# Issuing the second copy of x behind the stores instead of ahead of them, in a state-attention and Mish-MLP kernel

## The chip, the core and the metric

The kernel runs on one core of a Trainium2 chip. The metric is the device time of one launch in microseconds (us). The kernel before takes 706.17 us, the median of three runs (705.65 to 708.63). One further execution, of 704.28 us, was recorded by the hardware profiler; all profile lines are from it, and their times count from the start of its span of 702.3 us.

## The reference

Eight batches b of eight heads, each with 512 tokens of x (width 64) and 32 state rows. The tokens read from the state and the state reads from the tokens, by two softmaxes over the same scores; the results are stacked to 544 rows per batch and go through a two-layer network with the activation h * tanh(softplus(h)), called Mish.

```python
scores = scale * np.matmul(x, state.transpose(0, 1, 3, 2))
a = softmax(scores)                      # over the 32 state rows
xread = np.matmul(a, state)
scores2 = scale * np.matmul(state, x.transpose(0, 1, 3, 2))
a2 = softmax(scores2)                    # over the 512 tokens
sread = np.matmul(a2, x)
attn = np.concatenate([xread, sread], axis=2)      # (8, 8, 544, 64)
h = attn_as_rows @ w_in                  # (4352, 512) @ (512, 2048)
out = mish(h) @ w_out                    # (2048, 512)
```

Everything is float32 (softmax is short for the max, exp, sum and division of the reference).

## The kernel before, in words

**Work per batch.** `attention(b)` makes the softmax weights of batch b as pieces that are issued between the other work; a batch's attention runs one batch ahead. The network's hidden width of 2048 is cut into 8 slots `(b, j)` of two blocks of 128. In a slot, `sw_slice` (L377) multiplies the state into `w_in`, `gemm1` (L416) gives the 512 tokens' hidden values in two PSUM tiles `ph` (12 matmuls), ScalarE applies Mish (`g`, L394), VectorE splits `g` into `gh` and `gl` (L399, L400), and `gemm2` (L470, 24 matmuls) adds to four accumulators `acc` of 512 tokens in PSUM. Numbers are split into a high and a low part and multiplied in three matmuls. `gemm2` runs two slots behind `gemm1` (LAG).

**End of a batch.** After the eighth slot the four accumulators are copied to SBUF tiles `o` of which there are two: VectorE copies the even ones (L477), ScalarE the odd ones (L479), and SP issues a store of each to DRAM (L485). The third and fourth copy need a tile `o` whose store has landed. Because of the lag, this falls into slot 1 of the next batch.

**Two copies of x.** The token read needs x as it lies (`x`, L72, one tile). The scores need x transposed. For batches 0 and 1 TensorE transposes it. For batches 2 to 7 a second copy `xq` is loaded in blocks of 32x32 (L85, 32 DMAs of 32 KB for each batch), and VectorE transposes it in four instructions to `xT` (L197), one for each pair of heads c and c+4. The 32 DMAs go through the eight heads in turn, so chunk c of four is complete with DMA 20, 24, 28 or 32. `xq` takes a tile of the pool `raw` (two tiles, shared with the raw weights in the first batch, and with `ws` in the stage for the state rows, L432).

**What sets the order.** The Tile framework puts the program in order for each engine by a simulated timeline, and inserts the waits that the data and the buffers need. An engine's instructions then run in that order. `behind(m)` keeps what is issued in it from being placed before the instruction last marked `m`. All DMAs but three of the first state are issued from SP's one queue: a DMA there that waits for a buffer holds up all that stand behind it.

**Where `xq` is issued.** In the main loop, in batch `key`, `xq` of batch `key + 2` is issued in slots 6 and 7 (batch 0) or 2 to 5 (the others), behind the mark "mish", the last Mish activation.

In DMA and tile names a number after the name tells batches apart: `xq_1057` is batch 2, `xq_1371` batch 3, `xq_2026` batch 4; `o_0_1299` to `o_3_1326` are the results of batch 0, `o_0_1954` to `o_3_1981` of batch 1.

Of the kernel before, what the change touches and what calls it, by code (L numbers as in the profile page):

```python
# [39 lines left out]
def state_attention_mish_kernel(ctx, tc, x, state, w_in, w_out, out):  # L40

    nc = tc.nc
# [97 lines left out]
    def split_w_out(j, w):  # L140
        wo[j] = const.tile([P, 2, 2, DM], F32R, tag=f"wo{j}", name=f"wo_{j}")
        nc.vector.tensor_copy(wo[j][:, :, 1], w)
        last["wo"] = nc.vector.tensor_sub(wo[j][:, :, 0], w, as_f32(wo[j][:, :, 1]))  # L143
# [25 lines left out]
    last = {}  # L169

    @contextmanager
    def behind(*marks):

        with ExitStack() as st:
            for m in marks:
                st.enter_context(tc.issue_after(last[m].ins if hasattr(last[m], "ins") else last[m]))
            yield
# [228 lines left out]
    def gemm1(b, j, aT, sw):  # L406
        swh, swl = sw[j]
        phs = []
        for k in range(2):
            ph = ps_h.tile([P, 512], F32, tag="ph", name=f"ph_{b}_{j}_{k}")  # L410
            seq = []
            for kc in range(2):
                hi, lo = aT[kc]
                seq += [(swh[:, k, kc], hi), (swh[:, k, kc], lo), (swl[:, k, kc], hi)]
            for i, (l, r) in enumerate(seq):
                last["PE"] = nc.tensor.matmul(ph, l, r, start=(i == 0), stop=(i == len(seq) - 1))  # L416
            phs.append(ph)
        return phs
# [8 lines left out]
    def load_w_s(j):  # L427
        w = pool.tile([P, NC, 2, 2 * P], F32, tag="raw", name=f"ws_{j}", bufs=2)
        f0 = 2 * j * P
        for kc in range(2):  # L430
            for r in range(2):
                nc.sync.dma_start(  # L432
                    w[half(kc), :, r], w_in_sb[half(r), kc * NC:(kc + 1) * NC, f0:f0 + 2 * P])
        return w

    def gemm1_s(j, ws):

        g = new_g(f"s_{j}")
        ph = [ps_h.tile([P, 512], F32, tag="ph", name=f"ph_s_{j}_{r}") for r in range(2)]
        for r in range(2):  # L440
            for k in range(2):
                w = ws[:, :, r, k * P:(k + 1) * P]
                hi, lo = (pool.tile([P, NC, P], F32R, tag="t", name=f"w{n}_{j}_{r}_{k}", bufs=5) for n in "hl")
                nc.scalar.copy(hi, w)
                nc.vector.tensor_sub(lo, w, as_f32(hi))  # L445
                for c in range(NC):
                    for n, (l, i) in enumerate(((hi, 0), (hi, 1), (lo, 0))):
                        nc.tensor.matmul(  # L448
                            ph[r][:, k * 256:(k + 1) * 256], l[:, c], srT[i][:, c],
                            start=(c == 0 and n == 0), stop=(c == NC - 1 and n == 2))  # L450
        for r in range(2):
            take_g(g, r, ph[r])
        return split_g(f"s_{j}", g)
# [3 lines left out]
    def new_accs(key, ntok):  # L457
        accs[key] = [ps_acc.tile([P, 512], F32, tag="acc", name=f"acc_{key}_{t}") for t in range(ntok)]

    def gemm2(key, fcs, gh, gl, ntok, ts=None):  # L460

        if key not in accs:
            new_accs(key, ntok)
        for t in ts or range(ntok):
            for i, fc in enumerate(fcs):
                col = (i * ntok + t) * P
                sl = slice(col, col + P)
                ops = [(gh, 1), (gh, 0), (gl, 1)]
                for n, (g, w) in enumerate(ops):
                    last["PE"] = nc.tensor.matmul(  # L470
                        accs[key][t], g[:, sl], wo[fc % 8][:, fc // 8, w, :],
                        start=(fc == 0 and n == 0), stop=(fc == NFC - 1 and n == 2),
                    )
            if fcs[-1] == NFC - 1:
                o = pool.tile([P, DM], F32, tag="o", name=f"o_{key}_{t}")
                if t % 2 == 0:
                    nc.vector.tensor_copy(o, accs[key][t])  # L477
                else:
                    nc.scalar.copy(o, accs[key][t])  # L479
                if key == "s":  # L480
                    for b4 in range(4):
                        r0 = (4 * t + b4) * T + S
                        nc.sync.dma_start(out[r0:r0 + NS, :], o[b4 * NS:(b4 + 1) * NS, :])
                else:
                    nc.sync.dma_start(  # L485
                        out[key * T:key * T + S, :].rearrange("(p t) e -> p t e", t=NT)[:, t, :], o)


# [53 lines left out]
    def second(ts=None, keep=False):  # L542
        k_, fcs, g_, nt = pending[0] if keep else pending.pop(0)
        gemm2(k_, list(fcs), g_[0], g_[1], nt, ts)

    for n, (key, j) in enumerate(slots):
        if key == "s":
            if j == 0:
                ws_next = load_w_s(0)
            ws, ws_next = ws_next, load_w_s(j + 1) if j + 1 < 4 else None  # L550
            g = gemm1_s(j, ws)
            pending.append((key, (2 * j, 2 * j + 1, 2 * j + 8, 2 * j + 9), g, 2))
            second()
            continue
        if j == 0 and key > 0:
            aT = nxt_aT
        if key + 1 < B and j == (3 if key == 0 else 0):
            _, pcs, nxt_aT = attention(key + 1, xs_next, sn_next, xqs.pop(key + 1, None))
            todo += pcs
        phs = gemm1(key, j, aT, sw_next)  # L560
        if (key, j) == (0, 0):
            with behind("PE"):
                sw_next = sw_slice(0, 1, P)
            with behind("swl"):
                split_w_out(0, w_0)
            rawo.pop(0)
            with behind("swh", "wo"):
                g = mish(key, j, phs)
        else:
            g = mish(key, j, phs)  # L570
        pending.append((key, (j, j + 8), g, NT))
        if key == 0 and j + 1 < SLOTS:


            if j == 1:
                with behind("PE"):
                    second((0, 1), True)
            if j:
                with behind("PE"):
                    sw_next = sw_slice(0, j + 1, P)  # L580
            if j == 1:
                with behind("mish", "gl", "swh", "swl"):
                    rest[1]()
            with behind("mish", "gl", "swh", "swl", (0, "exp2") if j else "mish"):
                make(*makes.get(j, ()))
            if j == 0:
                with behind("join"):
                    rest[0]()
            if j == 0:
                with behind("PE"):  # L590
                    fills[0](FILL[2], accs[0][NT - 1])
                load(*((k, i) for i in range(3, 6) for k in "io" if (k, i) != ("i", 3)))
                with behind("load"):
                    xs_next, sn_next = load_x(1), load_state(1)
                load(*((k, i) for i in range(6, 8) for k in "io"))
            elif j == 1:
                with behind("PE"):
                    second((2, 3))
            elif j == 3:

                for do in (lambda: second((0, 1), True), todo.pop(0), lambda: second((2, 3))):
                    with behind("PE"):
                        do()
            elif j < 6:
                with behind("PE"):
                    second()
        else:
            nb, nj = (key, j + 1) if j + 1 < SLOTS else (key + 1, 0)
            if nb < B and nj % 2 == 0:
                sw_next = sw_slice(nb, nj)  # L610
        for _ in range((0, 0, 1, 1)[j] if key == 0 and j < 4 else 1 + (key == 0)):
            if todo:
                with behind(*(("PE",) if key == 0 and j == 2 else ())):
                    todo.pop(0)()
        if key + 2 < B and j in (parts := (6, 7) if key == 0 else (2, 3, 4, 5)):

            if j == parts[0]:
                xqs[key + 2] = new_xq(key + 2)
            m = 4 * H // len(parts)
            with behind("mish"):  # L620
                load_xq(key + 2, xqs[key + 2], range((j - parts[0]) * m, (j - parts[0] + 1) * m))
        if j == SLOTS - 1 and 0 < key + 2 < B:
            with behind("mish"):
                xs_next, sn_next = load_x(key + 2), load_state(key + 2)
        if len(pending) > LAG:
            second()
# [26 lines left out]
```

## Time and profile before

| what | value |
|---|---|
| median of three runs | 706.17 us (705.65 to 708.63) |
| the profiled execution, its span | 704.28 us, 702.3 us |
| TensorE matmul (PE) busy | 683.8 us, 97% |
| VectorE (DVE) busy | 341.5 us, 49% |
| ScalarE (ACT) busy | 263.8 us, 38% |
| GpSimd (POOL) busy | 10.4 us, 1% |
| mean granted TensorE clock | 0.994 |
| DMA, share of 16 engines | 26.3% for SP's queue |

The profile tells for each engine how long it was busy, which instruction ended an idle time ("idle before <-releaser"), and for DMAs when they were issued and how long they took to land. PEld is TensorE's weight load, SPq is SP issuing DMAs, DVEq and the like are the engines' sequencers. Matmuls overlap, so the start of one to the start of the next is the better measure of their pace.

### The profile page before, as it was taken

Reading aid. Unit: us, or ns where it says so; the run is one execution under the profiler, and the core shown is the slowest. Engines: PE = TensorE matmul, PEld = TensorE weight load, DVE = VectorE, ACT = ScalarE, POOL = GpSimd, SP = SyncE. Lnnn points to the kernel's source line nnn. Section 1 sums busy time; section 2 is a strip of 40 time slices with the busy share of each in tenths; the row PEclk is TensorE's granted clock in tenths of the full one; section 3 lists DMA queues with packets and bytes.
Section 4 is the critical chain, followed back from the end, with each engine's and each line's share of the span. In section 5 each row is a group of like instructions: output and inputs, shape, how many; then the busy total and the mean of one; then the engine's idle time right before and its main releaser. Section 6 shows DMA issues by size and latency. Waiting matters only on the chain.

```text
span 702.3 us, 11259 instructions
## 1 busy us (share of the span) xinstructions
PE 683.8 (97%) x4756; PEld 530.2 (75%) x4756; DVE 341.5 (49%) x517; ACT 263.8 (38%) x418; POOL 10.4 (1%) x13
## 2 busy tenths in 40 slices
PE   8889997999999999999999999999999999999997
PEld 6766775677777777787777777777777788977785
DVE  3687595375337533663258333743374324432221
ACT  5696853343126312451236122631245123222110
POOL 0110100000000000000000000000000000000000
PEclk9999999999999999999999999999999999999999
DMA  9995833520420032102310041004010007001001
GB/s 239 261 247 155 212 48 74 132 44 1 102 71 16 1 86 41 61 1 67 56 66 0 13 110 60 1 1 120 1 61 1 1 1 180 1 1 30 1 1 60
DMA packets 84529, 46.08 MB, mean 66 GB/s; under 512 B 57600, under 2 KB 78080, under 8 KB 84480
## 3 DMA queue, kind: packets, MB, share of 16 engines
q1 hardware_dynamic: 84048, 45.27, 26.3%
q8 instruction: 37, 0.61, 0.4%
q10 hardware_dynamic: 432, 0.10, 0.1%
q14 instruction: 12, 0.10, 0.0%
HBM read 32.24 MB, written 8.91 MB: 59 GB/s over the span
## 4 chain that ended last, share of the span: by engine, by line
PE 89%; DMA 4%; SPq 2%; DVE 2%; ACT 2%; issue 1%; ACTq 0%; DVEq 0%
PE acc L470 49%; PE ph L416 24%; PE swp L377 5%; PE ph_s L448 3%; PE acc_s L470 3%; DMA wir<-in_moe_w_in_dram 3%; SPq L85 2%; PE sc L216 1%; PE srp L327 1%; PE e2p L259 1%; DMA out_dram<-o 1%; DMA sn<-in_state_dram 1%; DVE wo L143 0%; PE xTp L203 0%; DVE w L106 0%
## 5 line engine op out<-in xcount | busy, mean ns | idle before, releaser
L470 PE MATMUL acc<-wo,gh 128*128 128x512 f32 x1024 | 328.8, 402 | 0.0
L470 PEld LDWEIGHTS acc<-wo,gh 128*128 128x128 f32 x1024 | 189.6, 189 | 55.4 <-issue 12.3
L470 PE MATMUL acc<-wo,gl 128*128 128x512 f32 x512 | 201.3, 396 | 0.0
L394 ACT ACTIVATE g<-ph 128x512 f32<-128x512 f32 x128 | 74.1, 597 | 228.6 <-DVE gl L400 162.6
L399 DVE CAST gh<-g 128x1024 fp32r<-128x1024 f32 x64 | 44.2, 691 | 158.6 <-PE acc L470 145.8
L470 PEld LDWEIGHTS acc<-wo,gl 128*128 128x128 f32 x512 | 96.8, 189 | 23.2 <-issue 0.4
L416 PE MATMUL ph<-ah,swh 128*128 128x512 f32 x256 | 101.9, 399 | 7.1 <-ACT swh L388 5.2
L416 PE MATMUL ph<-al,swh 128*128 128x512 f32 x256 | 102.2, 399 | 0.0
L416 PE MATMUL ph<-ah,swl 128*128 128x512 f32 x256 | 100.2, 397 | 0.0
L400 DVE TENSOR_TENSOR gl<-g,gh 128x1024 fp32r<-128x1024 f32 x64 | 79.0, 1234 | 5.0
L389 DVE TENSOR_TENSOR swl<-swp,swh 128x512 fp32r<-128x512 f32 (+1 forms) x72 | 42.9, 625 | 54.3 <-ACT swh L388 53.7
L416 PEld LDWEIGHTS ph<-ah,swh 128*128 128x128 f32 x256 | 48.4, 189 | 20.5 <-ACT swh L388 5.9
L416 PEld LDWEIGHTS ph<-al,swh 128*128 128x128 f32 x256 | 48.4, 189 | 11.6 <-DVE al L315 0.4
L416 PEld LDWEIGHTS ph<-ah,swl 128*128 128x128 f32 x256 | 48.3, 189 | 10.7 <-DVE swl L389 0.3
L388 ACT CAST swh<-swp 128x512 fp32r<-128x512 f32 (+1 forms) x72 | 35.8, 547 | 22.7 <-PE swp L377 22.7
L377 PE MATMUL swp<-w_in_sb,bd 64*32 64x256 f32 (+1 forms) x1152 | 40.8, 358 | 2.1 <-DVE rs L248 2.0
L394 ACT ACT_TABLE_LOAD x20 | 25.7, 1283 | 30.7 <-DVE gl L400 14.1
L377 PEld LDWEIGHTS swp<-w_in_sb,bd 64*32 64x32 f32 x1152 | 18.4, 106 | 20.5 <-issue 12.4
L479 ACT COPY o<-acc 128x512 f32<-128x512 f32 x16 | 9.4, 586 | 49.2 <-PE acc L470 27.5
L477 DVE COPY o<-acc 128x512 f32<-128x512 f32 x16 | 11.0, 688 | 28.3 <-DMA out_dram<-o 22.3
L445 DVE TENSOR_TENSOR wl<-ws,wh 128x512 fp32r<-128x512 f32 x16 | 11.1, 691 | 27.3 <-PE ph_s L448 23.3
L197 DVE STREAM_TRANSPOSE xT<-xq 128x512 f32<-128x512 f32 x24 | 24.3, 1092 | 0.0
(80 smaller groups left out, 527.5 us busy)
## 6 DMA issues: line engine op xcount, KB each, us to landing
x<-in_x_dram SPq DMA_DIRECT2D x32, 256.0 KB, 4.3
wir<-in_moe_w_in_dram SPq DMA_DIRECT2D x16, 512.0 KB, 9.3
wor<-in_moe_w_out_dram SPq DMA_DIRECT2D x16, 512.0 KB, 11.8
out_dram<-o SPq DMA_DIRECT2D x32, 256.0 KB, 2.4
xq<-in_x_dram SPq DMA_DIRECT2D x192, 32.0 KB, 2.3
ws<-w_in_sb SPq DMA_DIRECT2D x16, 256.0 KB, 4.3
sn<-in_state_dram SPq DMA_DIRECT2D x21, 32.0 KB, 3.0
out_dram<-o_s SPq DMA_DIRECT2D x8, 64.0 KB, 1.7
```

The costliest lines, as they stand in the source:

```text
L85: nc.sync.dma_start(xq[q * 32:(q + 1) * 32, h % NC, h // NC], x[b, h].rearrange("(i w u) d -> u i w d", w=8, u=2)[u][:, :, dh * 32:(dh + 1 ...
L197: nc.vector.transpose(xTs[c].rearrange("p (k v i g) -> p g k v i", k=2, v=2, g=4), xq[:, c].rearrange("p k (g v) d -> p g k v d", v=2))
L377: last["PE"] = nc.tensor.matmul(pw[r][o, kc * n:(kc + 1) * n], bds[b][half(r), kc ^ r, o], w_in_sb[half(r), kc * NC + c, j * P:j * P + n], ...
L388: last["swh"] = nc.scalar.copy(hr, pr)
L389: last["swl"] = nc.vector.tensor_sub(lo[:, r].rearrange("p k f -> p (k f)"), pr, as_f32(hr))
L394: last["mish"] = nc.scalar.activation(g[:, k * 512:(k + 1) * 512], ph, AF.Mish)
L399: nc.vector.tensor_copy(gh, g)
L400: last["gl"] = nc.vector.tensor_sub(gl, g, as_f32(gh))
L416: last["PE"] = nc.tensor.matmul(ph, l, r, start=(i == 0), stop=(i == len(seq) - 1))
L445: nc.vector.tensor_sub(lo, w, as_f32(hi))
L448: nc.tensor.matmul(ph[r][:, k * 256:(k + 1) * 256], l[:, c], srT[i][:, c], start=(c == 0 and n == 0), stop=(c == NC - 1 and n == 2))
L470: last["PE"] = nc.tensor.matmul(accs[key][t], g[:, sl], wo[fc % 8][:, fc // 8, w, :], start=(fc == 0 and n == 0), stop=(fc == NFC - 1 and ...
```

## The change

The stores of results get a mark of their own, "store". `xq` is then issued behind the last store that was issued, in batches 1 to 5 (so for batches 3 to 7), and behind the last load in batch 0 (for batch 2). By slot 2 of batch `key` the last store issued is that of the fourth tile of batch `key - 1`. No instruction is added or taken away, no size is changed.

```diff
@@ gemm2
                 else:
-                    nc.sync.dma_start(
+                    last["store"] = nc.sync.dma_start(
                         out[key * T:key * T + S, :].rearrange("(p t) e -> p t e", t=NT)[:, t, :], o)
@@ the main loop
             if j == parts[0]:
                 xqs[key + 2] = new_xq(key + 2)
             m = 4 * H // len(parts)
-            with behind("mish"):
+            with behind("store" if key else "load"):
                 load_xq(key + 2, xqs[key + 2], range((j - parts[0]) * m, (j - parts[0] + 1) * m))
```

The order on SP's queue, where batch 0 ends. Before (`xN` is a count of DMAs that stand together):

```order
L85 DMA xq_1057<-in_x_dram 32x8x32 x32
L85 DMA xq_1371<-in_x_dram 32x8x32 x24
L485 DMA out_dram<-o_0_1299 128x512
L485 DMA out_dram<-o_1_1308 128x512
L85 DMA xq_1371<-in_x_dram 32x8x32 x4
L485 DMA out_dram<-o_2_1317 128x512
L485 DMA out_dram<-o_3_1326 128x512
L85 DMA xq_1371<-in_x_dram 32x8x32
L72 DMA x_1157<-in_x_dram 128x2x256 x4
```

The same place on SP's queue with the change:

```order
L85 DMA xq_1057<-in_x_dram 32x8x32 x32
L153 DMA sn_1817<-in_state_dram 128x64 x3
L485 DMA out_dram<-o_1_1308 128x512
L485 DMA out_dram<-o_0_1299 128x512
L485 DMA out_dram<-o_2_1317 128x512
L485 DMA out_dram<-o_3_1326 128x512
L85 DMA xq_1371<-in_x_dram 32x8x32 x2
L72 DMA x_1157<-in_x_dram 128x2x256 x4
L85 DMA xq_1371<-in_x_dram 32x8x32 x30
```

All four stores of batch 0 now stand ahead of batch 3's `xq`; before, 24 of its DMAs stood ahead of the first two stores and four more ahead of the last two. Three small loads of a state (`sn`) moved ahead of the stores.

On VectorE one instruction changes its place, at the same point (piece of the difference):

```order
 L335 TENSOR_SCALAR srd_1055<-srp_0_1038,rs_0_962 128x64
 L197 STREAM_TRANSPOSE xT_3_1291<-xq_1057 128x4x128
+L477 COPY o_2_1317<-acc_2_194 128x512
 L389 TENSOR_TENSOR swl_0_1114<-swp_0_0_1095,swh_0_1113 128x512
-L477 COPY o_2_1317<-acc_2_194 128x512
 L389 TENSOR_TENSOR swl_0_1114<-swp_0_1_1096,swh_0_1113 128x512
```

The copy of the third result tile stands one instruction earlier, ahead of the low part `swl` of the first half of the weights for batch 1's slot 0. TensorE, ScalarE and GpSimd keep their order.

In the batches after it SP's queue now reads as here at the end of batch 1, with the change:

```order
L153 DMA sn_3127<-in_state_dram 128x64 x3
L485 DMA out_dram<-o_0_1954 128x512
L485 DMA out_dram<-o_1_1963 128x512
L485 DMA out_dram<-o_2_1972 128x512
L485 DMA out_dram<-o_3_1981 128x512
L85 DMA xq_2026<-in_x_dram 32x8x32 x32
L72 DMA x_2467<-in_x_dram 128x2x256 x4
L153 DMA sn_3782<-in_state_dram 128x64 x3
```

Before, batch 4's `xq_2026` and batch 5's `xq_2681` both stood ahead of batch 1's stores, and batch 6's `xq_3336` right behind them; now each batch's `xq` stands behind the stores of the batch three before it.

## The prediction

> **What bounds the kernel now.** I read the page's busy times first, then who waits for whom, then the timeline of the one place where TensorE waits.
>
> ```profile
> PE 683.8 (97%) x4756; PEld 530.2 (75%) x4756; DVE 341.5 (49%) x517; ACT 263.8 (38%) x418; POOL 10.4 (1%) x13
> ```
>
> TensorE is the bound, and only time in which it stands still or runs slowly can be won. Its waits between 113 and 640 us are one row:
>
> ```profile
> PE ph L416 <- ACT swh L388: 3.9, 1, 3.9
> ```
>
> The rest of that stretch is full (busy time by stage; the first number behind the stretch's length is PE):
>
> ```profile
> 130.00:140.00 10.00, 10.00 (x66) 6.14 (x65) 3.21 (x4) 2.59 (x5) 0.00 (x0) 1.00 0.37 63
> 250.00:326.00 76.00, 76.00 (x526) 58.41 (x525) 37.35 (x59) 25.90 (x43) 0.00 (x0) 1.00 0.18 44
> 580.00:640.00 60.00, 60.00 (x360) 50.26 (x359) 22.40 (x29) 16.78 (x29) 0.00 (x0) 1.00 0.25 62
> ```
>
> So what the change can win lies at that one wait, at the start of batch 1. Its chain, from TensorE backwards. TensorE's timeline there:
>
> ```profile
> 119.18 0.39 PE L416 MATMUL ph<-al,swh 128*128 128x512 f32 x1
> 119.41 0.40 PE L416 MATMUL ph<-ah,swl 128*128 128x512 f32 x1
> 123.68 0.77 PE L416 MATMUL ph<-ah,swh 128*128 128x512 f32 x1 [3.87 <-ACT swh L388]
> 124.25 0.63 PE L416 MATMUL ph<-al,swh 128*128 128x512 f32 x1
> ```
>
> ScalarE's:
>
> ```profile
> 112.83 0.59 ACT L479 COPY o<-acc 128x512 f32<-128x512 f32 x1 [1.26 <-PE acc L470]
> 122.56 0.58 ACT L479 COPY o<-acc 128x512 f32<-128x512 f32 x1 [7.05 <-DMA out_dram<-o]
> 123.04 0.59 ACT L388 CAST swh<-swp 128x512 fp32r<-128x512 f32 x1
> ```
>
> VectorE's:
>
> ```profile
> 113.83 0.68 DVE L477 COPY o<-acc 128x512 f32<-128x512 f32 x1
> 115.54 0.70 DVE L389 TENSOR_TENSOR swl<-swp,swh 128x512 fp32r<-128x512 f32 x1
> 121.95 0.69 DVE L477 COPY o<-acc 128x512 f32<-128x512 f32 x1 [5.72 <-DMA out_dram<-o]
> ```
>
> And SP's:
>
> ```profile
> 77.06 42.27 SPq L85 DMA_DIRECT2D xq<-in_x_dram  x56
> 119.43 1.02 SPq L485 DMA_DIRECT2D out_dram<-o  x2
> ...
> 123.14 1.02 SPq L485 DMA_DIRECT2D out_dram<-o  x2
> ...
> 124.87 2.11 SPq L72 DMA_DIRECT2D x<-in_x_dram  x4
> ...
> 130.53 22.20 SPq L85 DMA_DIRECT2D xq<-in_x_dram  x32
> ...
> 198.67 1.50 SPq L153 DMA_DIRECT2D sn<-in_state_dram  x3
> 206.00 4.20 SPq L485 DMA_DIRECT2D out_dram<-o  x4
> ```
>
> The weights' second half `swh`, for which TensorE waits, stands on ScalarE behind the copy of result tile 3. That copy waits 7.05 us for a tile `o` whose store has not landed. The first two tiles were copied by 113.42 and 114.51, but SP was issuing `xq` until 119.33 and issued their stores only then; the waiting copies start 2.5 and 3.1 us later, against a landing time of:
>
> ```profile
> DMA to landing us min/median/max: 2.1/2.4/4.1
> ```
>
> The store is late because of the 24 DMAs of batch 3's `xq` ahead of it, and for no other reason that the trace shows. Later batches have their stores on time: at 206.00 SP had been free since 200.17 (198.67 + 1.50).
>
> **The change part by part.** *The idle time, removed.* Matmuls start 0.23 us apart (119.18 to 119.41), so the next was due at 119.64 and came at 123.68: 4.04 us. With the change SP is free at this point: it has 32 DMAs of batch 2's `xq` (at 0.755 us each, 42.27/56, they fill 77.06 to about 101) and the three of `sn_1817`, bounded from below by nothing and from above by the slow first rate, 3 x 0.755 = 2.3 us; done by 104, nine us before the first store is wanted. I walk the chain with durations of the rows above and a landing of 2.5 us:
> - store of tile 1, issued at 113.4, lands at 115.9; VectorE's copy of tile 2 (now ahead of `swl`) runs 115.9 to 116.6, the first `swl` 116.6 to 117.3;
> - store of tile 0, issued at 114.5, lands at 117.0; ScalarE's copy of tile 3 runs 117.0 to 117.6, `swh` 117.5 to 118.1, the second `swl` 118.1 to 118.8.
>
> What TensorE wants, and when:
>
> ```profile
> 116.38 1.07 PE L377 MATMUL swp<-w_in_sb,bd 64*32 64x256 f32 x16
> 118.03 0.65 PE L327 MATMUL srp<-x,e2T 128*32 128x64 f32 x32
> 118.61 0.50 PE L416 MATMUL ph<-ah,swl 128*128 128x512 f32 x1
> ```
>
> The accumulators are complete before 116.38, so the copies don't wait for them. `srp` at 118.03 takes the PSUM buffer that the first `swl` reads: free at 117.3, slack 0.7 us. The matmul due at 119.64 needs `swh`: there at 118.1, slack 1.5 us. So this wait goes wholly: **4.04 us**.
>
> *The slow restart, removed with it.* By stage, with the granted clock as the third number from the end:
>
> ```profile
> 123.68:126.90 3.22, 3.22 (x10) 2.48 (x10) 0.86 (x2) 2.13 (x3) 0.00 (x0) 0.51 0.69 201
> 126.90:130.00 3.10, 3.10 (x18) 2.33 (x20) 2.36 (x4) 0.74 (x3) 0.00 (x0) 0.96 1.02 312
> ```
>
> Matmuls that started every 0.23 us start every 0.43 to 0.57 us (123.68, 124.25). At a clock of 0.51, 3.22 us hold 1.58 us too much; at 0.96, 3.10 us hold 0.12 us: **1.70 us**. Without the idle time there is nothing for the clock to drop on.
>
> *What comes after.* Mish, `gh`, `gl` and the next weights follow TensorE's own results there, so they come earlier with it. VectorE and ScalarE had 5.72 and 7.05 us of idle time at this very place, which they now get back as earlier work. I find no further wait in walking to 128 us: Mish of the first `ph` ends at 120.4 (table load behind `swh`, 118.1 to 119.4), and its buffer is wanted at 121.4. I take 0. The lower bound of this term is 0, as no row shows TensorE idle that could be filled; the upper one is rival 1 below.
>
> *`xq` of batch 3, moved back.* 32 DMAs and the four of `x` go behind the stores: from about 118 at 22.20/32 = 0.69 us, plus 2.1 us for `x`, issued by 143, landed by 145.5. It is wanted at:
>
> ```profile
> 159.26 3.00 DVE L197 STREAM_TRANSPOSE xT<-xq 128x512 f32<-128x512 f32 x3
> 231.42 2.96 DVE L197 STREAM_TRANSPOSE xT<-xq 128x512 f32<-128x512 f32 x3
> 237.44 0.69 DVE L399 CAST gh<-g 128x1024 fp32r<-128x1024 f32 x1 [3.06 <-PE acc L470]
> 249.07 1.08 DVE L197 STREAM_TRANSPOSE xT<-xq 128x512 f32<-128x512 f32 x1
> ```
>
> 159.26 less 5.7 is 153.5: hidden, with 8 us to spare. Its cover are VectorE's instructions up to there.
>
> *`xq` of batches 4 to 7, moved back.* This is where the change costs cover. The stores of batch 1 are issued by 210.2 (all times of both shift alike). Chunk 2 is complete with DMA 28: 210.2 + 28 x 0.694 + 2.3 = 231.9. VectorE turns to it as its third transpose, at 231.42 + 2 x 0.99 = 233.4. Chunk 0 (DMA 20) is there at 226.4, chunk 3 (DMA 32) at 234.7 for 249.07. So 1.5 us to spare in the tightest, and behind it VectorE idles 3.06 us anyway. The landing of 2.3 us is the median here:
>
> ```profile
> DMA to landing us min/median/max: 2.1/2.3/8.2
> ```
>
> Price 0, as long as that cover holds. `x` and `sn` behind `xq` wait for buffers that come free at the same times as before, and are consumed a batch later; `ws`, the first of which moves behind batch 7's `xq`, is wanted only in the stage of the state rows, more than a batch later.
>
> *Sum.* 4.04 + 1.70 = 5.74 us. The profiled execution of 704.28 us becomes 698.5 us. The median of the three runs stands 1.89 us above that execution, so the forecast for the median is 706.17 - 5.74 = **700.4 us**. For this kernel, a change under 0.5% (3.5 us) can't be told from none; 5.7 us is 0.8%.
>
> **Rivals.** *1. A shorter wait in the same place.* VectorE's copy of tile 2 now stands ahead of `swl`, so a late store holds up both `swl` and `srp`. If stores land in their maximum of 4.1 us instead of 2.5, `swl` ends at 118.9 and `srp` is 0.9 us late, and `swh` is there at 119.8, 0.1 us late. TensorE loses about 1.0 us: 701.4 us. If the clock also drops, 1.70 us more, 703.1 us. For it: the pool's rotation ties two engines to two stores. Against it: no `xq` competes with these stores any longer. Whether the clock drops after a short wait is seen earlier in the trace:
>
> ```profile
> 44.57 0.67 PE L377 MATMUL swp<-w_in_sb,bd 64*32 64x128 f32 x32 [2.04 <-DVE rs L248]
> 44.00:46.00 2.00, 1.43 (x34) 1.17 (x35) 1.62 (x3) 1.97 (x3) 0.00 (x0) 0.81 0.91 297
> 46.00:48.00 2.00, 2.00 (x6) 1.52 (x6) 1.37 (x3) 1.98 (x5) 0.00 (x0) 0.50 0.98 247
> 107.99 0.66 PE L259 MATMUL e2p<-ident,e 128*128 128x128 f32 x4 [0.70 <-ACT e L245]
> 100.00:120.00 20.00, 19.11 (x166) 13.50 (x164) 14.22 (x27) 8.45 (x14) 0.00 (x0) 1.00 0.31 48
> ```
>
> A wait of 2.04 us was followed by a clock of 0.50, one of 0.70 us by none (1.00 over the 20 us). 1.0 us is nearer the latter, so 701.4 is the likelier of the two. The Trainium skill, TensorE: Matmul & The Clock Gate, section "What's actually happening", has the clock halved after an idle window of about 3.4 us; by it a wait of 1.0 us would cost no clock, and rival 1 would end at 701.4 alone. The trace agrees on the half (0.51 after 3.87 us) and not on the length (0.50 after 2.04 us).
>
> *2. The gain is given back.* VectorE and ScalarE, which caught up during the stall, turn out to be just in time behind it, and TensorE waits in pieces in batch 1 or later: 0 to 4 us of the 5.74 remain, 702 to 706, say 705 us. For it: VectorE has much to do between 140 and 160 (softmax of batch 2). Against it: nothing on TensorE waits in 130 to 640 us, and VectorE idles 8.13 us in front of that softmax:
>
> ```profile
> 142.41 1.31 DVE L291 STREAM_TRANSPOSE e<-scs 128x512 f32<-128x512 f32 x2 [8.13 <-ACT scs L224]
> ```
>
> *3. Not the queue.* If the copies waited for something else than the late issue, the stores would come early and the copies would not: 706 us. Against it stand the 2.5 us from issue to release.
>
> *4. Slower: `xq` late in batches 4 to 7.* VectorE runs in order; if chunk 2 is not there when it turns to it, `gh` and `gl` behind it are late, then Mish, then TensorE. With the slow issue of 0.755 us and a landing of 8.2 us (its maximum), chunk 2 is there at 210.2 + 21.1 + 8.2 = 239.5, 6.1 us late; 3.06 us are VectorE's idle time, and 3 us in each of four batches, 12 us, would reach TensorE if `gemm2`'s lag of two slots hid nothing: 700.4 + 12 = 712 us. It decides from a delivery after 236.5. For it: 1.5 us of spare time by the medians is little. Against it: later issues are at 0.694 or faster, and nothing else is on the queue then. The Trainium skill, Perfetto Trace Analysis, section "DMA Optimizations", suggests one issuing engine for inputs and another for outputs; by it loads behind stores on one queue are what to avoid, and rival 4 is how that would cost here. No run so far shows it.
>
> **How the numbers follow.** Forecast (both terms, no new wait) 0.74; rival 1 0.12, rival 2 0.08, rival 3 0.02, rival 4 0.04. Around the forecast the three runs before spread from 0.5 us below to 2.5 us above their median. Range 698.8 to 703.8: it holds the forecast with that spread, nearly all of rival 1 and a part of rival 2. Faster by over 0.5% means below 702.6: 0.72 from the forecast, 0.08 from rival 1: 0.80. Slower means above 709.7: 0.03 to 0.04, from rival 4. The rest, 0.16, is no change.
>
> **What would show it.** Right: stores of batch 0 issued at about 113.4 and 114.5; no TensorE wait over 1 us after 113; a granted clock of 1.00 from 118 to 130; the end of the span near 696.5; `xq` of batch 4 issued in one block right behind the stores of batch 1, and its transposes without an idle time in front that a DMA ends. Wrong: an idle time before `srp` or `ph` at 117 to 121 (rival 1), ScalarE or VectorE released by a store there (rival 3), TensorE waits spread over later batches (rival 2), or a row in which VectorE's `xT` waits for a DMA of `xq` and TensorE waits a few us later (rival 4).

## The result and the profile after

| | before | with the change |
|---|---|---|
| median of 10 runs on one chip | 705.29 us (702.1 to 708.63) | 699.16 us (696.36 to 702.1) |
| ratio, 95% interval | | 0.9917 (0.9891 to 0.9942) |
| the profiled execution, its span | 704.28 us, 702.3 us | 696.36 us, 694.6 us |

The change makes the kernel faster by 0.8%, and the interval leaves out 1. Two repetitions (e8, e11 below) gave 0.9911 and 0.9910. One execution of the kernel before, of 2835 us beside e1 to e4, is left out of their ratios. The forecast was 5.74 us of 706.17 us, a ratio of 0.9919. The time forecast, 700.4 us, lies 1.2 us above the measured one, of which 0.9 us is that the kernel before has a lower median over these ten runs than over the three before the prediction.

TensorE's waits are read first. This view of the kernel with the change lists who waited for whom between 40 and 130 us (us in total, how often, the longest):

```profile
PE swp L377 <- DVE rs L248: 2.0, 1, 2.0
PE ph L416 <- ACT swh L388: 1.3, 1, 1.3
PE e2p L259 <- ACT e L245: 0.7, 1, 0.7
```

All three come before 113 us and stand in the kernel before too. From 113 to 640 us the same view has no row at all; before it had one, of 3.9 us. SP's timeline of the kernel with the change (start, length, what is issued, how many):

```profile
111.07 4.20 SPq L485 DMA_DIRECT2D out_dram<-o  x4
115.32 1.24 SPq L85 DMA_DIRECT2D xq<-in_x_dram  x2
116.66 2.08 SPq L72 DMA_DIRECT2D x<-in_x_dram  x4
118.79 20.12 SPq L85 DMA_DIRECT2D xq<-in_x_dram  x30
...
197.92 4.27 SPq L485 DMA_DIRECT2D out_dram<-o  x4
202.24 21.42 SPq L85 DMA_DIRECT2D xq<-in_x_dram  x32
```

The stores now go out as soon as their tile is copied, and `xq` follows in one block. ScalarE and VectorE at the same place, with the change:

```profile
110.45 0.59 ACT L479 COPY o<-acc 128x512 f32<-128x512 f32 x1 [1.27 <-PE acc L470]
112.54 0.59 ACT L388 CAST swh<-swp 128x512 fp32r<-128x512 f32 x1 [1.49 <-PE swp L377]
114.33 0.59 ACT L479 COPY o<-acc 128x512 f32<-128x512 f32 x1 [1.20 <-DMA out_dram<-o]
115.13 0.59 ACT L388 CAST swh<-swp 128x512 fp32r<-128x512 f32 x1 [0.22 <-PE swp L377]
```

```profile
111.46 0.67 DVE L477 COPY o<-acc 128x512 f32<-128x512 f32 x1
113.28 0.69 DVE L477 COPY o<-acc 128x512 f32<-128x512 f32 x1
113.89 0.68 DVE L389 TENSOR_TENSOR swl<-swp,swh 128x512 fp32r<-128x512 f32 x1
```

ScalarE's copy of tile 3 waits 1.20 us for a store instead of 7.05, and the `swh` behind it waits for its own input. VectorE's copy of tile 2 has no idle time in front. TensorE is full from there on, at full clock (the first number behind the stretch's length is PE, the third from the end the granted clock):

```profile
113.00:120.00 7.00, 7.00 (x73) 4.85 (x72) 3.30 (x7) 3.94 (x7) 0.00 (x0) 1.00 0.64 202
120.00:130.00 10.00, 10.00 (x66) 6.37 (x65) 4.74 (x7) 2.77 (x5) 0.00 (x0) 1.00 0.46 97
140.00:640.00 500.00, 500.00 (x3396) 389.79 (x3395) 234.98 (x364) 168.31 (x283) 0.00 (x0) 1.00 0.17 43
```

**Where the 7.7 us between the two spans come from.** Not all of it is the change's. TensorE's timeline of the kernel before, then with the change, at matching places (more of the same view of the kernel before stands in the prediction):

```profile
68.63 0.50 PE L416 MATMUL ph<-ah,swh 128*128 128x512 f32 x1 [1.34 <-ACT swh L388]
...
126.87 0.61 PE L416 MATMUL ph<-ah,swh 128*128 128x512 f32 x1
...
697.52 0.40 PE L470 MATMUL acc<-wo,gl 128*128 128x512 f32 x1
```

```profile
43.98 0.67 PE L377 MATMUL swp<-w_in_sb,bd 64*32 64x128 f32 x32 [2.00 <-DVE rs L248]
66.45 0.50 PE L416 MATMUL ph<-ah,swh 128*128 128x512 f32 x1 [1.34 <-ACT swh L388]
...
117.03 0.40 PE L416 MATMUL ph<-ah,swl 128*128 128x512 f32 x1
...
118.89 0.49 PE L416 MATMUL ph<-ah,swh 128*128 128x512 f32 x1
...
689.43 0.40 PE L470 MATMUL acc<-wo,gl 128*128 128x512 f32 x1
```

At 44 us the second execution is ahead by 0.59 us (44.57 less 43.98), and at 67 us by 2.18. Nothing that the change moves has run by then. At the last matmul ahead of the old wait it is ahead by 2.38 (119.41 less 117.03), at the next slot (126.87 less 118.89) by 7.98. From there on the lead is 8.09: at VectorE's `gh` (237.44 less 229.35) and still at the last matmul of the launch (697.52 less 689.43). So the stretch with the old wait gave 8.09 - 2.38 = **5.71 us**, and of the 2.4 us won earlier 2.2 can't be the change's. Behind the last matmul the execution with the change takes 0.4 us longer (5.17 against 4.78), which leaves the 7.7 us. For 1.6 us of the early lead the cause is seen: both executions wait 2.0 us at 44 us, but only the one before is granted half the clock afterwards (0.50 between 46 and 48 us). With the change that stretch reads:

```profile
46.00:48.00 2.00, 2.00 (x11) 1.60 (x10) 1.88 (x4) 1.97 (x5) 1.19 (x1) 1.00 1.08 245
```

The medians, over ten runs each, differ by 6.1 us; such chances weigh less in them.

**A correction to the description ahead of the prediction.** It says that `behind(m)` keeps an instruction from being placed before the one marked `m`. In these programs it does so only where both run on the same engine. The old mark "mish" is on a ScalarE instruction and held no DMA of SP: in the profile before, 28 of batch 3's 32 DMAs are issued by 123.1 us, and the first Mish of batch 1 starts at 124.94. That is why this `xq`, which the program issues in slots 2 to 5 of batch 1, could stand ahead of batch 0's stores, which belong to slot 1. The new mark is on an SP instruction, and with it all 32 stand behind the stores.

### The profile page after: what moved, and what is told of

Read it like the earlier page. It is cut to its first block, busy times and chain, and to the rows that moved or that the text cites. A ratio compares the mean times of both kernels' runs of the same rounds, so it can differ in the third digit from the quotient of the medians.

```text
span 694.6 us, 11259 instructions
## 1 busy us (share of the span) xinstructions
PE 680.6 (98%) x4756; PEld 528.3 (76%) x4756; DVE 341.8 (49%) x517; ACT 263.9 (38%) x418; POOL 10.8 (2%) x13
## 4 chain that ended last, share of the span: by engine, by line
PE 90%; DMA 4%; ACT 2%; DVE 2%; issue 1%; SPq 0%; POOL 0%; DVEq 0%; ACTq 0%; POOLq 0%
PE acc L470 50%; PE ph L416 24%; PE swp L377 5%; PE ph_s L448 3%; PE acc_s L470 3%; DMA wir<-in_moe_w_in_dram 3%; PE sc L216 1%; PE srp L327 1%; DMA wor<-in_moe_w_out_dram 1%; PE e2p L259 1%; PE warm L184 1%; DVE w_in_sb L106 1%; PE xTp L203 0%; ACT L394 0%; DMA out_dram<-o 0%
## 5 line engine op out<-in xcount | busy, mean ns | idle before, releaser
L394 ACT ACT_TABLE_LOAD x20 | 25.7, 1283 | 30.7 <-DVE gl L400 14.1
```

The source lines that it names most:

```text
L394: last["mish"] = nc.scalar.activation(g[:, k * 512:(k + 1) * 512], ph, AF.Mish)
```

## The experiments

They ran in three sets on three chips (e1 to e4; e5 to e8; e9 to e11), each set beside executions of the kernel before, whose median was 704.56, 705.6 and 704.54 us. So the ratios are compared, not the times.

**e1 and e2: the change for one batch alone, and for the others alone.** e1 keeps the new mark for batch 3's `xq` only, e2 for those of batches 4 to 7 only.

```diff
-            with behind("store" if key else "load"):
+            with behind("store" if key == 1 else "mish"):      # e1
+            with behind("store" if key > 1 else "mish"):       # e2
```

> Only batch 3's xq stands behind batch 0's stores; batches 4 to 7 as before. Theory (the whole gain is the one stall where batch 0 ends, 4.04 us of idle time and 1.70 us of slow clock): ratio to the kernel before 0.992, and TensorE waits nowhere after 113 us. Rival (the later batches' queue order has a part in it): 0.995 to 1.000.

> Only the xq of batches 4 to 7 stand behind the stores; batch 3's stands ahead of batch 0's stores as before. Theory: ratio 1.000, the wait of 3.9 us for swh is still there. Rival (the later batches' queue order has a part in it): 0.992 to 0.997.

Measured: e1 698.51 us, ratio 0.9929 (0.9895 to 0.9963); e2 705.65 us, 1.0013 (0.9988 to 1.0038). In e1 TensorE has no wait from 113 to 640 us. In e2 the old wait stands where it was, for the same instruction. It is longer than the 3.9 us of before because TensorE was there 1.0 us earlier (its last matmul ahead of the wait started at 118.39, not 119.41) while SP issued the first two stores no earlier (119.48, not 119.43). TensorE's waits in that stretch of e2, and the clock behind it:

```profile
PE ph L416 <- ACT swh L388: 5.2, 1, 5.2
```

```profile
124.00:127.20 3.20, 3.20 (x9) 2.47 (x10) 0.85 (x2) 2.08 (x3) 0.00 (x0) 0.50 0.75 220
```

What follows: within these intervals the whole gain is batch 3's `xq` behind batch 0's stores, and moving the `xq` of batches 4 to 7 gives nothing and costs nothing. e1 leaves batch 2's `xq` at its old mark too, so the new mark "load" is not needed for the gain.

**e3: the crowded queue stays, the copies get other tiles.** SP's order is that of before. The copies of tiles 2 and 3 of batch 0 go to two tiles that lie idle at that time, so they need no landed store (the store is L491 here, the copies L483 and L485).

```diff
+                if key == 0 and t == 2:
+                    o2.append(pool.tile([P, 2, DM], F32, tag="wt", name="o2", bufs=1))
+                if key == 0 and t > 1:
+                    o = o2[0][:, t - 2]
+                else:
+                    o = pool.tile([P, DM], F32, tag="o", name=f"o_{key}_{t}")
```

> The queue as before (24 DMAs of batch 3's xq ahead of batch 0's stores), but result tiles 2 and 3 of batch 0 are copied to a tile of the weights' pool that lies idle there, so that their copies need no store to have landed. Theory (the stall is the copies' wait for a tile): ratio 0.992 although SP issues batch 0's stores as late as before, at about 117 to 120 us. Rival (a late store or a crowded queue costs by itself, by its traffic or by what stands behind it): 1.000.

Measured: 698.57 us, ratio 0.9919 (0.9887 to 0.9951), no wait of TensorE from 113 to 640 us. SP's queue and ScalarE in e3:

```profile
99.92 21.28 SPq L85 DMA_DIRECT2D xq<-in_x_dram  x31
121.30 1.02 SPq L491 DMA_DIRECT2D out_dram<-o  x2
```

```profile
117.39 0.59 ACT L485 COPY o<-acc 128x512 f32<-128x512 f32 x1 [0.98 <-PE acc L471]
118.42 0.58 ACT L388 CAST swh<-swp 128x512 fp32r<-128x512 f32 x1 [0.44 <-PE swp L377]
```

The stores are as late as ever (121.30), and it costs nothing: ScalarE's copy of tile 3 now waits for the accumulator alone. So late stores, and 24 DMAs ahead of them, are harmless by themselves. The cost is the chain from the store through the tile `o` to the copy, with `swh` behind that copy on ScalarE. It can be cut at either end, with the same gain within the intervals.

**e4 and e5: how much may stand ahead of the stores.** With the change's order, 18 or 28 of the 32 DMAs of batch 3's `xq` are issued ahead of batch 0's stores, the rest behind them. (Before, it was 24, and four more ahead of the last two stores.)

```diff
+        if (key, j) == (1, 0):
+            xqs[3] = new_xq(3)
+            load_xq(3, xqs[3], range(18))     # e4; e5: range(28)
...
+                    with behind(*(("xq",) if key == 0 else ())):     # around the store; "xq" marks L85
```

> 18 of batch 3's 32 xq DMAs (and three small state loads) ahead of batch 0's stores, the other 14 behind; all other engines in the order of the changed kernel. Theory: on the axis of the profile before, the stores go out at 102.8 + 18 x 0.69 + 1.7 = 116.9 us, tile 3's copy starts at 119.9 and swh is there at 121.0, so TensorE waits about 1.4 us instead of 3.9. If the clock does not drop after so short a wait, ratio 0.994; if it drops as after 3.9 us, 0.9963. Rival (the stall is not set by the number of DMAs ahead): 0.992 or 1.000.

> 28 of batch 3's xq DMAs ahead of batch 0's stores. The copies of tiles 2 and 3 now stand one instruction later, behind the second swh and swl, so the late store holds up the Mish of batch 1's first slot in place of swh. Theory: stores at 102.8 + 28 x 0.69 = 122.1 us on the axis of the profile before, tile 3's copy at 125.2, table load and Mish to 127.7; TensorE, whose next ph is due at 121.4, waits about 6 us for it, and with the slow clock that is 7.5 to 8 us over the changed kernel: ratio to before 1.003. Rival (the stall is full at 24 and more DMAs add nothing): 1.000 or less.

Measured: e4 702.2 us, 0.9974 (0.9947 to 1.0002); e5 708.07 us, 1.0039 (1.0007 to 1.0071). The more stands ahead, the longer the time: 0.9917 with none, 0.9974 with 18, 1 as before, 1.0039 with 28. The number is not all that differs, as the order on the other engines is not the same in all four. e4 costs more than was expected, and in another place: the expectation followed the late store to `swh` and left out `srp`, which rival 1 had named. VectorE's, SP's and TensorE's timelines of e4 (L486 is the store, moved by a line):

```profile
117.44 0.69 DVE L477 COPY o<-acc 128x512 f32<-128x512 f32 x1 [3.41 <-DMA out_dram<-o]
118.05 0.68 DVE L389 TENSOR_TENSOR swl<-swp,swh 128x512 fp32r<-128x512 f32 x1
```

```profile
113.44 1.50 SPq L153 DMA_DIRECT2D sn<-in_state_dram  x3
115.04 3.93 SPq L486 DMA_DIRECT2D out_dram<-o  x4
```

```profile
118.88 1.08 PE L327 MATMUL srp<-x,e2T 128*32 128x64 f32 x32 [2.47 <-DVE swl L389]
```

The stores start 4.0 us later than with the change (115.04 against 111.07; 0.7 of it is that this execution is later throughout), VectorE's copy of tile 2 waits for one, `swl` stands behind that copy, and `srp` needs the buffer that `swl` reads. That is rival 1, place and chain, though not in the change itself. e4 has VectorE's copy of tile 2 ahead of both `swl`, as the change has, so this new place on VectorE does not remove the stall by itself. TensorE ran at about half clock afterwards:

```profile
118.90:122.20 3.30, 3.30 (x38) 2.71 (x39) 0.98 (x2) 1.59 (x3) 0.00 (x0) 0.54 0.67 199
```

2.47 us of wait and 3.30 x 0.46 = 1.52 us of slow clock make 4.0 us; the ratio stands 0.0057 above the change's, 4.0 us of 705. That they agree so closely is luck, since each ratio is uncertain by about 2 us. In e5 the order on VectorE and ScalarE is another again (the copies one instruction later). TensorE's waits there between 113 and 640 us:

```profile
PE srTp L339 <- DVE srd L335: 4.9, 1, 4.9
PE ph L416 <- ACT g L394: 1.2, 1, 1.2
```

They are 6.1 us together, with a clock of 0.50 in the 6.5 us from 123.50 on. The ratio and the length of the wait came as expected (1.003, 6 us), but not the place: Mish was to be all of it and is 1.2 us of it. The victim is whatever the scheduler puts behind the waiting copy: `swh` before, `swl` and `srp` in e4, `srd` and Mish in e5.

**e6 and e9: the stores on another engine's queue.** SP keeps its `xq` as before; the 32 stores of the token results are issued by ScalarE (e6) or by GpSimd (e9).

```diff
-                    last["store"] = nc.sync.dma_start(
+                    nc.scalar.dma_start(       # e6; e9: nc.gpsimd.dma_start
```

> The kernel before with the stores of the token results issued from ScalarE's queue, xq as before on SP's. Theory: the stores go out as the copies end, whatever SP does, so the wait of 3.9 us is gone: ratio 0.992. Rival (issuing 32 stores, each waiting for VectorE's copy, holds up ScalarE's in-order work, swh and Mish): 0.995 to 1.005, with TensorE waiting for swh or g in every batch.

> The kernel before with the stores of the token results issued from GpSimd's queue, whose DMAs have semaphores of their own, so that a store waits for nothing of SP's (ScalarE's stores did: they share SP's ring of eight semaphores, and the first store waited 5.7 us for an xq to land). Theory: the copies of batch 0's tiles 2 and 3 no longer wait 7 us, TensorE waits less than 1 us there: ratio 0.992 to 0.995, the last store of the kernel perhaps 1 to 2 us slower from GpSimd. Rival (the stores' queue is not what counts): 1.000.

Measured: e6 703.95 us, 0.9988 (0.996 to 1.0015), so the expected gain did not come. ScalarE's timeline in e6 (ACTq is ScalarE issuing DMAs):

```profile
115.60 1.60 ACTq L485 DMA_DIRECT2D out_dram<-o  x2
117.24 0.58 ACT L388 CAST swh<-swp 128x512 fp32r<-128x512 f32 x1 [5.71 <-DMA xq<-in_x_dram]
120.34 0.34 ACTq L485 DMA_DIRECT2D out_dram<-o  x1
120.78 0.58 ACT L479 COPY o<-acc 128x512 f32<-128x512 f32 x1 [2.95 <-DMA xq<-in_x_dram]
```

ScalarE stands still for a DMA of `xq`, with which a store has nothing to do by its data. The program's instructions say why; these are two of ScalarE's rows with what they wait for:

```
L485 DMA out_dram<-o_1_1308 128x512 [waits DMAHW1_49,Activation_49]
L485 DMA out_dram<-o_0_1299 128x512 [waits DMAHW3_49,DVE_49]
```

In this program the DMAs of SP and of ScalarE share eight completion semaphores (DMAHW0 to 7), and a new DMA waits for the earlier one on its semaphore (a semaphore is the counter by which a DMA reports that it has landed). So the store, and all of ScalarE behind it, waits for an `xq` that SP has issued. TensorE loses 2.32 us at `ph` and 1.28 us at `srp`, and runs at 0.50 from 120 to 124 us. The time is the rival's, but not for the rival's reason: from 113 us on TensorE has no other wait, in no later batch.

e9 gave 701.33 us, 0.9961 (0.9935 to 0.9987). GpSimd's DMAs have eight semaphores of their own in this program (DMASW0 to 7). SP still has 41 `xq` DMAs in a row, but the stores do not wait for them: the first one is released by its tile's copy. TensorE stays full at full clock. SP, GpSimd (POOL) and TensorE's stretch in e9:

```profile
99.62 29.20 SPq L85 DMA_DIRECT2D xq<-in_x_dram  x41
```

```profile
115.04 0.71 POOL L485 DMA_DIRECT2D out_dram<-o  x1 [26.34 <-ACT o L479]
```

```profile
113.00:135.00 22.00, 22.00 (x198) 14.42 (x197) 11.68 (x18) 7.76 (x13) 2.33 (x4) 1.00 0.54 137
```

So this too removes the stall, but half of the gain is gone. Part of it is at the launch's end. In e9 the last matmul starts at 693.11 us of 700.4, with the change at 689.43 of 694.6: 7.3 against 5.2 us behind it. VectorE's last copy starts 0.56 us behind the last matmul's start in e9 (693.67), and with it in the change (689.42); the rest of the 2.1 us lies behind that copy. The ratios are 0.0044 apart, 3.1 us; the last 1 us was not traced. In that profile the weights `wir` of the first stage also land later (median 14.1 us; the other profiles have 8.9 to 12.9), and whether this belongs to e9 or to chance is open. The Trainium skill, Perfetto Trace Analysis, section "DMA Optimizations", suggests one engine for loads and another for stores. Here that is worth nothing that could be measured on ScalarE, and half as much as the new order on GpSimd.

**e7 and e10: `xq` made late.** Rival 4 hung on how late `xq` of batches 4 to 7 may come. With the change's order each of those DMAs is split in two of 16 KB, so that each `xq` needs 64 issues.

```diff
+            for w in ((slice(0, 4), slice(4, 8)) if b > 3 else (slice(0, 8),)):
+                nc.sync.dma_start(
+                    xq[q * 32:(q + 1) * 32, h % NC, h // NC, w],
+                    x[b, h].rearrange("(i w u) d -> u i w d", w=8, u=2)[u][:, w, dh * 32:(dh + 1) * 32])
```

> The changed kernel with each xq DMA of batches 4 to 7 split in two of 16 KB, which doubles SP's issue time to about 41 us a batch; the data are the same. This prices the rival that forecast a loss: chunk 0 lands at about 230 us against VectorE's turn at 223.3, chunk 2 at about 240 against 225.3. If VectorE's order passes the lateness on, gl and swl of slots 4 to 6 come 7 to 12 us late and TensorE waits 4 to 6 us in each of four batches, ratio to before 1.015 to 1.025. If the lag of two slots hides it, 0.992.

Measured: 696.97 us, ratio 0.9877 (0.9844 to 0.991). SP and VectorE in e7:

```profile
202.60 32.39 SPq L86 DMA_DIRECT2D xq<-in_x_dram  x64
```

```profile
224.55 1.10 DVE L198 STREAM_TRANSPOSE xT<-xq 128x512 f32<-128x512 f32 x1 [0.79 <-DMA xq<-in_x_dram]
228.55 1.09 DVE L198 STREAM_TRANSPOSE xT<-xq 128x512 f32<-128x512 f32 x1 [2.89 <-DMA xq<-in_x_dram]
231.85 1.13 DVE L198 STREAM_TRANSPOSE xT<-xq 128x512 f32<-128x512 f32 x1 [1.45 <-DMA xq<-in_x_dram]
232.79 1.23 DVE L401 TENSOR_TENSOR gl<-g,gh 128x1024 fp32r<-128x1024 f32 x1
```

```profile
113.00:640.00 527.00, 527.00 (x3623) 407.82 (x3623) 249.32 (x385) 176.53 (x298) 0.00 (x0) 1.00 0.19 46
```

VectorE waits 5.1 us for `xq` in this batch alone. It takes the third chunk 6.2 us later than with the change, where the three transposes run together from 223.33 on (e7's execution is 0.36 us later here throughout): that is the lateness of 6.1 us with which rival 4 reckoned. `gl` starts 2.3 us later (230.15 with the change), as VectorE's idle time and an order with `gh` ahead of the third transpose take up the rest. TensorE is busy in all of 527 us. So the first half of rival 4 is real, and the second is not: `gl` is ready at 234.0, and TensorE reads it two slots on, from 243.46. The next work that hangs on VectorE's order is `swl` for the `gemm1` at 239.24, ready at 237.0, 2.2 us early. The issues took 32.4 us and not the 41 of the expectation, so its 7 to 12 us of delay were not reached; a delay some 3 us longer than here might have stopped TensorE, which no run shows.

The ratio is the best of all, though nothing in the profile explains a gain from the split. So it was run again, beside the change.

> The split xq of batches 4 to 7 again, beside the change itself on the same chip. If its 697.0 us against the change's 699.4 were the chance of the clock's drops in the first 80 us, the two are the same within 0.3% now, and each kernel's single times fall with its mean clock; if the split itself saves time, it is 0.3% faster again.

> The change beside the split xq on the same chip. Theory: ratio to before 0.992; the same as the split within 0.3%.

Measured: e10 698.24 us, 0.9915 (0.9885 to 0.9945); e11, the change, 697.6 us, 0.9910 (0.9875 to 0.9944). The split is no faster than the change, so e7's lower ratio did not repeat. The mean clock fits that: e7's six executions had 0.998 to 1.000, those of the change beside it (e8) 0.995 to 0.997. In the last set both kernels have values from 0.995 to 1.000.

**e8: the change once more.**

> The change once more, for a second profile beside these runs. Theory: ratio 0.992, no TensorE wait over 1 us after 113 us. Open is the slow clock after the 2.0 us wait near 44 us, which the profile before shows and the first profile of the change does not: if it comes and goes from one execution to the next with the wait unchanged, it is no part of the change's gain.

Measured: 699.42 us, 0.9911 (0.9878 to 0.9944). No wait of TensorE from 113 to 640 us. This profile, of the same program as the first, has the half clock after the 2.0 us wait that the first one has not:

```profile
44.22 0.67 PE L377 MATMUL swp<-w_in_sb,bd 64*32 64x128 f32 x32 [2.01 <-DVE rs L248]
```

```profile
46.00:48.00 2.00, 2.00 (x6) 1.57 (x5) 1.65 (x2) 1.98 (x4) 1.19 (x1) 0.50 1.01 243
```

No version beats the change beyond its scatter; e3 equals it.

## Why the prediction was right

- **The chain at batch 1's start** (stores late behind `xq`, copies waiting for a tile, `swh` behind the copy): right in every link. e2 keeps the stall with the queue, e1 removes it with the queue, e3 removes it with the queue left as it was.
- **4.04 us of idle time and 1.70 us of slow restart, 5.74 us**: 5.71 us between the two profiles, and by the ratios 0.8 to 0.9% against the 0.8% forecast. The restart was rightly counted in: without it the forecast would have been 0.57%, and e4 shows the two parts side by side. That the two spans differ by 7.7 us, 2 us more, is chance.
- **The walk to the stores**: forecast at 113.4 and 114.5 by the clock of the trace before, issued from 111.07 on, which is 113.45 with the 2.38 us by which this execution was ahead. The landing of 2.5 us was a little long: VectorE's copy of tile 2 (forecast 115.9) ran at 113.28, 115.66 on that clock, without waiting, and ScalarE's copy of tile 3 (forecast 117.0) at 114.33, 116.71 on that clock.
- **Nothing given back behind it (0)**: right, 500 of 500 us busy from 140 to 640 us, and the lead of 8.09 us is kept to the last matmul. Rival 2 falls. Rival 3 falls too: with early stores the copies start early, and in e3 copies that need no store start without waiting for one.
- **`xq` at a price of 0**: right, and by more than was thought. By the same working as in the prediction, chunk 2 of batch 4 lands at 202.24 + 28 x 0.669 + 2.3 = 223.3 and is wanted as the third transpose of this row with the change:

```profile
223.33 2.96 DVE L197 STREAM_TRANSPOSE xT<-xq 128x512 f32<-128x512 f32 x3
```

  That is at 225.3: 2.0 us to spare against the 1.5 us forecast, as the issues took 0.669 us each and not 0.694. And e7 shows that this spare time is not what decides.
- **Rival 1**: did not occur. `swl` was through at 114.57, 1.1 us ahead of `srp` (115.65). But the order of the slacks was right (`srp` would suffer before `swh`), as e4 shows at 2.47 us. Its clock-free form was held the likelier because 1.0 us is short; that stays open, as no run had a wait that short there.
- **Rival 4**: its price was wrong. Delivery past 236.5 was to cost TensorE 3 us in each batch, 12 us in all. On e7's clock, which is about 7.7 us ahead there, that point is 228.8; the last of the three chunks was taken at 231.85, 3 us past it, and TensorE lost nothing. What the rival had wrong is that VectorE's delay reaches TensorE undiminished. Its condition, that the lag of two slots hides nothing, did not hold: in e7 `gl` was ready 9.4 us before TensorE read it.
- **The end of the span near 696.5**: 694.6, 697.6 and 694.6 in the three profiles of the change. The two lower ones lack the half clock at 44 us, on which the change has no influence; the higher one has it there and again behind a wait near 67 us. So how near 696.5 a single profile comes is luck.

## What to carry to other kernels

A DMA queue is a list in order, and a store of results behind a block of loads can stop a busy engine through the buffer that it would have set free: look in the waits for a copy released by a store, then on the queue for what was issued ahead of that store. Price such a stall with the slow restart behind it, and follow what stands behind the waiting copy in each order, since the scheduler may change what is held up (`swh`, `srp`, `srTp` in three orders here). Either a better order on the queue or a spare buffer ends it; another engine's queue did so only where its DMAs shared no semaphores with the first, and the gain was half.

## What the runs showed of the hardware

**A wait of 2.0 us drops the clock in some executions and not in others.** All 13 profiles, all kernels together, have the wait for `rs` at 44 us. Eleven of them have it at 1.99 to 2.05 us: two (before, e8) were granted 0.50 between 46 and 48 us, nine 1.00. The two with a longer one, 2.24 us in e3 and 2.27 us in e9, were granted 0.53 and 0.50. The five with a wait of 2.3 us or more at the start of batch 1 (before, e2, e4, e5, e6) all ran at about half clock behind it. Near 67 us nine have a wait of 1.34 us, and one of them (e8) ran at half clock behind it; so did e1, which has two waits there, of 1.39 and 0.49 us, within 2 us. So in these profiles every wait from 2.2 us on was followed by a drop, and of the shorter ones a few. The prediction's reading that 2.04 us make the clock drop was one draw of this. The Trainium skill, TensorE: Matmul & The Clock Gate, section "What's actually happening", has a window of about 3.4 us that runs free of the kernel. That the same wait sometimes drops the clock agrees with a free-running window; that 1.34 us was enough in e8 does not agree with a whole window of idleness.

**A drop costs 1.5 us or more beside the wait.** It cost 1.6 us at 44 us before and 1.5 us in e4, and e5 had a clock of 0.50 over 6.5 us. With one or two such chances in a launch, the ten times of the change differ by 5.7 us (696.36 to 702.1); the two runs of the change with a mean clock of 1.000 took 696.4 and 697.1 us, the three with 0.995 took 699.8 to 701.1. It is not the whole of the spread: one with 0.997 took 702.1. So differences below 1% need medians of several runs, and a pair of profiles needs its clock looked at, stage by stage, before a difference is put down to a change.

**SP's issue of a DMA takes three quarters of the time for half the bytes**: 0.51 us for 16 KB (32.39/64 in e7) and 0.67 us for 32 KB (21.42/32 with the change). So cutting a load in two makes its issue longer, here from 21.4 to 32.4 us.
